# A decode kernel's five engine programs: in the bodies of a block, or straight in the main block

## The chip, the cores and the metric

The kernel runs on one core of a Trainium2 chip. Its time is the device time of one execution in microseconds (us). The profile's *span* is something else: it runs from the first to the last instruction of the program. What comes after the last instruction is in the time and not in the span (447.38 us against a span of 445.6 in the profiled execution of before). Some executions of this program fall into a slower state near 447 us; those are left out of every comparison of times. The one profile of the kernel before is of such a slow execution; where a reading rests on it, a fast profile is set beside it.

## The reference, cut to what matters

One decode step for 8 requests, condensed here: an adaptive layer norm whose six modulation vectors come from `silu(c) @ w_mod`, a grouped-query attention over a cache of 8192 keys and values (32 query heads, 4 key/value heads), and a gated feed-forward network.

```python
def reference(A_x, A_k_cache, A_v_cache, A_wq, A_wo, B_x, B_W_gate, B_W_up, B_W_down, c, w_mod):
    mod = (silu(c) @ w_mod).reshape(8, 6, 1, -1)             # sa, ca, ga, sb, cb, gb
    h = layernorm(A_x) * (1 + ca) + sa
    x = A_x + ga * attention(h, A_k_cache, A_v_cache, A_wq, A_wo)
    h = layernorm(x) * (1 + cb) + sb
    return x + gb * (relu(h @ B_W_gate) * (h @ B_W_up)) @ B_W_down
    # ... cut: the functions' bodies; all inputs and the output are bf16
```

Nearly all the data is read once: 185.63 MB from HBM, most of it the two caches.

## The kernel before: the parts that the argument touches

The kernel records every operation with what it reads and writes. `plan` turns dependencies into semaphore waits, and `emit` writes one engine's instructions.

```python
class Prog:
    ENGINES = ("sp", "act", "pool", "dve", "pe")
    # ... cut: op() finds each operation's dependencies, plan() numbers the semaphores
    def emit(self, eng, e, sems):
        known = {}
        for o in self.ops:
            if o["eng"] != eng:
                continue
            # ... cut: want = the semaphore values that o waits for
            for s, v in sorted(want.items(), key=str):
                if known.get(s, 0) < v:
                    known[s] = v
                    e.wait_ge(sems[s], v)
            # ... cut: the instructions themselves, and the increment of the last
```

Loads are issued by SyncE into a ring in SBUF; a load waits until the ring slot that it overwrites has been read. At the end of the program the result is stored by four DMAs, two issued by SyncE and two by ScalarE. SyncE then waits for all four. The last operation is empty: only its waits are emitted.

```python
        for j in range(4):
            P.op("sp" if j % 2 == 0 else "act",
                 lambda e, j=j: e.dma_start(o2[:, 256 * j:256 * (j + 1)], ob[32 * j:32 * j + B, :]),
                 reads=[R("ob")], writes=[("out", j, j + 1)], dma=True)
        P.op("sp", [], reads=[("out", 0, 4)])

        P.plan()
        block = E(nc.Block())
        bass_engs = {"sp": nc.sync, "act": nc.scalar, "pool": nc.gpsimd, "dve": nc.vector, "pe": nc.tensor}
        starters = {"sp": block.sync, "act": block.scalar, "pool": block.gpsimd, "dve": block.vector, "pe": block.tensor}
        for name in P.ENGINES:
            def body(_, name=name):
                P.emit(name, bass_engs[name], sems)
            starters[name](body)
```

`nc.Block()` gives each engine a body of its own. In the built program each engine has a branch into its body, a branch from the body's end to a common end block, and there a barrier of all engines: a drain and a semaphore wait on each, with GpSimd gathering the arrivals and releasing the rest.

Of the kernel before, what the change touches and what calls it, by code (L numbers as in the profile page):

```python
# [132 lines left out]
def bass_adaLN_cond__gqa_block_cached__glu_gated_reglu__decode_kernel(nc, A_x, A_k_cache, A_v_cache, A_wq, A_wo, B_x, B_W_gate, B_W_up, B_W_down, c, w_mod, out):  # L133
    B, _, D = A_x.shape
    _, G, Sk, Dh = A_k_cache.shape
# [16 lines left out]
    P = Prog()  # L152
    with ExitStack() as es:
        E = es.enter_context
# [50 lines left out]
        sems = {("eng", e): E(nc.semaphore("s_" + e)) for e in P.ENGINES}  # L205
# [417 lines left out]
        P.op("sp", [], reads=[("out", 0, 4)])  # L623

        P.plan()
        block = E(nc.Block())
        bass_engs = {"sp": nc.sync, "act": nc.scalar, "pool": nc.gpsimd, "dve": nc.vector, "pe": nc.tensor}
        starters = {"sp": block.sync, "act": block.scalar, "pool": block.gpsimd, "dve": block.vector, "pe": block.tensor}
        for name in P.ENGINES:
            def body(_, name=name):  # L630
                P.emit(name, bass_engs[name], sems)
            starters[name](body)


# [26 lines left out]
```

## Time and profile before

| | before |
|---|---|
| first three timed runs, us | 446.92, 439.91, 440.66 |
| profiled execution, us | 447.38, slow; span 445.6 |
| DMA | 185.90 MB at 417 GB/s over the span |

These lines of the page of the profiled execution of before say what bounds it. The digits of the DMA row are the busy share of the 16 DMA engines in tenths, in 40 equal slices of the span.

```profile
span 445.6 us, 4024 instructions
...
DMA  8999999999999999999999999999999999999994
...
DMA 48%; DVE 25%; PE 23%; ACT 2%; issue 1%; SPq 0%
...
L428 DVE STREAM_TRANSPOSE kt<-arena 128x1024 uint32<-128x1024 uint32 x128 | 148.6, 1215 | 44.6 <-DMA arena<-in_A_k_cache_dram 41.8
L439 PE MATMUL ps<-kt,qpad 128*128 128x512 bf16 x512 | 121.7, 382 | 12.7 <-DVE kt L428 10.8
```

The line with percentages is the chain of work that ended last. The lines of groups have busy us, mean ns of one instruction, then idle us before them and what ended it. The DMA engines are busy nearly throughout, and loads alternate on the chain with the work that frees their slots. Branches and barriers are not counted as work anywhere on this page.

The barriers do show among the waits of SyncE's queue in before: engine and line, what it waited for, total us, times, longest.

```profile
SPq L237 <- PE ps L482: 199.7, 16, 13.3
...
SPq L621 <- DVE ob L616: 34.2, 1, 34.2
...
SPq L123 <- DMA out_dram<-ob: 1.1, 2, 0.9
SPq L646 <- PEq L646: 0.7, 1, 0.7
SPq L153 <- PEq L153: 0.2, 1, 0.2
```

L123 is the wait for the stored result. L646 is the barrier at the start, which belongs to the launch code and not to the block. L153 is the end of the block. All instructions of the end of the block, in the trace of before, by source line (durations in ns, start of first and last in us):

```profile
L153 POOLq EVENT_SEMAPHORE  x2: 17/17/17, 445.4 to 445.5; - x2
L153 POOLq DRAIN  x1: 1024/1024/1024, 333.8 to 333.8; - x1
L153 PEldq DRAIN  x1: 462/462/462, 441.9 to 441.9; - x1
L153 DVEq DRAIN  x1: 464/464/464, 442.8 to 442.8; - x1
L153 ACTq DRAIN  x1: 234/234/234, 444.2 to 444.2; - x1
L153 SPq COMPARE_BRANCH  x1: 33/33/33, 445.2 to 445.2; - x1
L153 SPq DRAIN  x1: 7/7/7, 445.4 to 445.4; - x1
L153 SPq EVENT_SEMAPHORE  x1: 17/17/17, 445.5 to 445.5; - x1
L153 ACTq EVENT_SEMAPHORE  x1: 17/17/17, 445.5 to 445.5; - x1
L153 DVEq EVENT_SEMAPHORE  x1: 21/21/21, 445.5 to 445.5; - x1
L153 PEldq EVENT_SEMAPHORE  x1: 51/51/51, 445.5 to 445.5; - x1
```

### The profile page before, as it was taken

Reading aid. Unit: us, or ns where it says so; the run is one execution under the profiler, and the core shown is the slowest. Engines: PE = TensorE matmul, PEld = TensorE weight load, DVE = VectorE, ACT = ScalarE, POOL = GpSimd, SP = SyncE. Lnnn points to the kernel's source line nnn. Section 1 sums busy time; section 2 is a strip of 40 time slices with the busy share of each in tenths; the row PEclk is TensorE's granted clock in tenths of the full one; section 3 lists DMA queues with packets and bytes.
Section 4 is the critical chain, followed back from the end, with each engine's and each line's share of the span. In section 5 each row is a group of like instructions: output and inputs, shape, how many; then the busy total and the mean of one; then the engine's idle time right before and its main releaser. Section 6 shows DMA issues by size and latency. Waiting matters only on the chain.

```text
span 445.6 us, 4024 instructions
## 1 busy us (share of the span) xinstructions
PE 273.7 (61%) x1691; PEld 121.9 (27%) x1691; DVE 262.9 (59%) x372; ACT 28.8 (6%) x48; POOL 19.9 (4%) x77
## 2 busy tenths in 40 slices
PE   0054347585775959577595867769595875564235
PEld 0021112222332423333242333324233332351112
DVE  0233028396878769687885967788686878521020
ACT  1100010201001010110101011010101001100000
POOL 6000010000000000000000000000000000000000
PEclk9997557796969789696987969688796988867555
DMA  8999999999999999999999999999999999999994
GB/s 353 427 388 384 379 379 403 390 424 447 434 429 429 425 444 435 426 432 427 439 434 429 435 425 438 435 429 431 429 434 439 432 429 426 436 429 431 435 419 194
DMA packets 6946, 185.90 MB, mean 417 GB/s; under 512 B 816, under 2 KB 912, under 8 KB 1168
## 3 DMA queue, kind: packets, MB, share of 16 engines
q1 hardware_dynamic: 6896, 185.64, 98.4%
q8 instruction: 13, 0.21, 0.2%
q14 instruction: 5, 0.04, 0.0%
q10 hardware_dynamic: 32, 0.01, 0.0%
HBM read 185.63 MB, written 0.02 MB: 417 GB/s over the span
## 4 chain that ended last, share of the span: by engine, by line
DMA 48%; DVE 25%; PE 23%; ACT 2%; issue 1%; SPq 0%
DMA arena<-in_A_k_cache_dram 33%; DVE kt L428 14%; PE ps L482 11%; DMA arena<-in_B_W_down_dram 8%; PE ps L439 8%; DMA arena<-in_w_mod_dram 7%; DVE pT L473 4%; DVE negm L446 3%; ACT prb L466 2%; PE ps L571 1%; PE ps L352 1%; PE ps L452 1%; PE ps L592 1%; DVE mj L457 1%; DVE kt L561 0%
## 5 line engine op out<-in xcount | busy, mean ns | idle before, releaser
L428 DVE STREAM_TRANSPOSE kt<-arena 128x1024 uint32<-128x1024 uint32 x128 | 148.6, 1215 | 44.6 <-DMA arena<-in_A_k_cache_dram 41.8
L439 PE MATMUL ps<-kt,qpad 128*128 128x512 bf16 x512 | 121.7, 382 | 12.7 <-DVE kt L428 10.8
L482 PE MATMUL ps<-arena,pT 128*64 128x512 bf16 x512 | 92.1, 539 | 50.5 <-DVE pT L473 50.5
L482 PEld LDWEIGHTS ps<-arena,pT 128*64 128x64 bf16 x512 | 44.3, 153 | 92.9 <-issue 87.3
L439 PEld LDWEIGHTS ps<-kt,qpad 128*128 128x128 bf16 x512 | 45.1, 97 | 87.8 <-DVE kt L428 32.3
L473 DVE STREAM_TRANSPOSE pT<-prb 64x1024 bf16<-64x1024 bf16 x32 | 39.6, 1239 | 15.9 <-ACT prb L466 15.4
L466 ACT ACTIVATE prb<-ps,bias 128x1024 bf16<-128x1024 f32 x16 | 17.8, 1114 | 276.3 <-DVE mjt L460 276.3
L446 DVE TENSOR_REDUCE negm<-ps 128x1 f32<-128x512 f32 x32 | 22.0, 686 | 10.7 <-PE ps L439 10.5
L421 POOL COPY qpad<-qR 32x32 bf16<-32x32 bf16 x64 | 13.1, 204 | 314.0 <-PE ps L439 255.4
L592 PE MATMUL ps<-arena,hT 128*32 128x448 bf16 x128 | 11.2, 522 | 15.9 <-DMA arena<-in_B_W_gate_dram 6.8
L452 PE MATMUL ps<-identf,negm 128*128 128x128 f32 x32 | 7.8, 325 | 15.7 <-DVE negm L450 15.7
L495 DVE SCALAR_TENSOR_TENSOR om<-ps,im,om 128x128 f32<-128x128 f32 x48 | 16.7, 348 | 0.6
L375 PE MATMUL ps<-arena,hT 128*32 128x512 bf16 x64 | 7.2, 631 | 14.7 <-DMA arena<-in_A_wq_dram 14.7
L599 DVE TENSOR_TENSOR kt<-ps,kt 128x448 bf16<-128x448 f32 x2 | 1.2, 620 | 25.0 <-PE ps L592 25.0
L500 PE MATMUL ps<-jmp,om 128*128 128x16 f32 x32 | 6.5, 280 | 14.7 <-DVE om L495 14.7
L290 DVE CAST cxr<-ps 128x512 bf16<-128x512 f32 x1 | 0.7, 692 | 19.2 <-PE ps L288 19.2
L288 PE MATMUL ps<-cx,rsel 32*128 32x512 bf16 x1 | 0.6, 581 | 18.6 <-DMA cx<-in_A_x_dram 18.6
L385 DVE CAST kt<-ps 128x512 bf16<-128x512 f32 x1 | 0.7, 693 | 18.3 <-PE ps L375 18.3
L610 PE MATMUL ps<-arena,kt 128*32 128x256 bf16 x112 | 6.9, 416 | 7.4 <-DMA arena<-in_B_W_down_dram 7.3
L452 PEld LDWEIGHTS ps<-identf,negm 128*128 128x128 f32 x32 | 4.7, 187 | 23.6 <-DVE negm L450 22.1
L352 PE MATMUL ps<-arena,hT 128*32 128x512 bf16 x96 | 9.0, 553 | 2.4 <-DMA arena<-in_w_mod_dram 2.4
L592 PEld LDWEIGHTS ps<-arena,hT 128*32 128x32 bf16 x128 | 4.2, 129 | 22.2 <-DMA arena<-in_B_W_up_dram 8.3
(80 smaller groups left out, 95.7 us busy)
## 6 DMA issues: line engine op xcount, KB each, us to landing
arena<-in_A_k_cache_dram SPq DMA_DIRECT2D x16, 4096.0 KB, 28.9
arena<-in_A_v_cache_dram SPq DMA_DIRECT2D x16, 4096.0 KB, 25.7
arena<-in_w_mod_dram SPq DMA_DIRECT2D x2, 6144.0 KB, 17.4
arena<-in_A_wq_dram SPq DMA_DIRECT2D x2, 4096.0 KB, 25.0
arena<-in_A_wo_dram SPq DMA_DIRECT2D x2, 4096.0 KB, 27.5
arena<-in_B_W_gate_dram SPq DMA_DIRECT2D x2, 3584.0 KB, 30.5
arena<-in_B_W_up_dram SPq DMA_DIRECT2D x2, 3584.0 KB, 33.5
arena<-in_B_W_down_dram SPq DMA_DIRECT2D x1, 3584.0 KB, 36.1
```

Source lines behind the costliest of these rows:

```text
L352: fns.append(lambda e, w=w, pr=pr, j=j, kk=kk: e.matmul(ps[32 * j:32 * j + 32, pr, :], hT[:, kk, :], w[:, 2 * pr:2 * pr + 2, j, :], start= ...
L375: fns.append(lambda e, w=w, z=z, g=g, kk=kk: e.matmul(ps[32 * g:32 * g + 32, 3 + z, :], hT[:, kk, :], w[:, g, z, :], start=(kk == 0), stop ...
L421: P.op("pool", lambda e, n=2 * m + Q // 2, Q=Q: e.tensor_copy(qpad[32 * Q:32 * Q + 32, m % 2, :, 24 + 32 * Q:32 + 32 * Q], qR[32 * Q:32 * ...
L428: P.op("dve", lambda e: e.transpose(ktb[:, to:to + QE].bitcast(dt.uint32), arena[:, lo:lo + QE].bitcast(dt.uint32)), reads=[slot_r(lo, lo ...
L439: fns.append(lambda e, t=t, r=r: e.matmul(ps[:, b, :].rearrange("p (c k) -> p c k", k=32), qpad[:, m % 2, t * 2 + r, 24 - 8 * i:152 - 8 * ...
L446: P.op("dve", lambda e: e.tensor_reduce(negm[:, h:h + 1], ps[:, b, :], AX.X, ALU.max, negate=True), reads=[bank(b)], writes=[R("negm", h, ...
L452: P.op("pe", lambda e: e.matmul(ps[:, 4, 0:128], negm[:, 2:3].to_broadcast([128, 128]), identf[:], start=True, stop=True), reads=[R("negm" ...
L466: P.op("act", lambda e: e.activation(prb[:], ps[:, 2 * z:2 * z + 2, :].rearrange("p h n -> p (h n)"), ACT.Exp, bias=bias[:, z:z + 1], scal ...
L473: P.op("dve", lambda e, g=g: e.transpose(pT[64 * g:64 * g + 64, z, :, g, :], prb[64 * g:64 * g + 64, :]), reads=[R("prb"), R("pT", z, z + ...
L482: fns.append(lambda e, t=t: e.matmul(ps[64 * (t % 2):64 * (t % 2) + 64, 5, :].rearrange("p (i d) -> p i d", d=Dh), pT[:, z, t].rearrange(" ...
L495: P.op("dve", lambda e, i=i: e.scalar_tensor_tensor(out=om[:], in0=ps[:, 5, Dh * i:Dh * i + Dh], scalar=im[:, i:i + 1], in1=om[:], op0=ALU ...
L592: fns.append(lambda e, w=w, r=kk - r0, kk=kk, h=h, j=j, b0=b0: e.matmul(ps[32 * j:32 * j + 32, b0 + h, 0:H], hT[:, kk, :], w[:, r, j, h, : ...
```

## The change

The intent is to do without branches and without the barrier at the end. The program is the same otherwise: per engine, the same instructions in the same order.

```diff
         P.plan()
-        block = E(nc.Block())
-        bass_engs = {"sp": nc.sync, "act": nc.scalar, "pool": nc.gpsimd, "dve": nc.vector, "pe": nc.tensor}
-        starters = {"sp": block.sync, "act": block.scalar, "pool": block.gpsimd, "dve": block.vector, "pe": block.tensor}
-        for name in P.ENGINES:
-            def body(_, name=name):
-                P.emit(name, bass_engs[name], sems)
-            starters[name](body)
+        for name, e in (("sp", nc.sync), ("act", nc.scalar), ("pool", nc.gpsimd), ("dve", nc.vector), ("pe", nc.tensor)):
+            P.emit(name, e, sems)
```

## The prediction

> **What bounds the kernel now.** The span of the profiled run is 445.6 us (a slow-state run; timed: 439.91, 440.66 and one slow 446.92). The page gives 185.90 MB at a mean of 417 GB/s, DMA busy 8 or 9 tenths in 39 of 40 slices. The chain of what ended last is DMA 48%, DVE 25%, PE 23%: loads and the transposes and matmuls that free their ring slots take turns. "Issue" is 1%. No view gives a share to a branch or barrier; the change touches nothing of this bound.
>
> **What changes.** The comparison of the built programs shows the same instructions in the same order on each engine; the changed one lacks one unconditional branch per engine at the start, one at the end, and the end barrier (a drain and a semaphore wait on each engine, GpSimd gathering and releasing). The barrier at the start is not the block's, and stays. SyncE's waits for the four output DMAs stay as plain waits; the last rode on its branch. Nothing is added.
>
> **Cost at the end.** In the trace's instruction records SyncE's last output wait, on its branch, starts at 445.213 us and is done at 445.246; its drain is at 445.369, GpSimd's gather at 445.401, its release at 445.485, and the last engine leaves at 445.59. So 0.34 us follow the last output wait, all on the critical path. (The waits view has 0.2 us for SyncE there.) The other engines reach the barrier earlier (ScalarE's drain is done at 444.46), so their branches cost nothing. The runtime's own barrier afterwards (semaphore updates from 445.83 to 446.36), resets, and a second barrier until 447.51 stay.
>
> **Cost at the start.** SyncE's release from the first barrier ends at 0.673 us and its first load issues at 0.739: 0.066 us hold the branch and the issue gap. [...] TensorE's first matmul waits until 18.60 us for small input loads, so its branch is free.
>
> **Sum.** [...] From fast runs at about 440.3 I predict 439.9 us, range 438.8 to 443.0: run-to-run spread and a mix with slow-state runs exceed the effect. Chances: faster by over 2% 0.01, within 2% 0.97, slower 0.02.
>
> **What would show it.** SyncE's output wait is the last instruction, no end drain or gather; from last output DMA issue to the span's end about 0.35 us shorter; first load issue near 0.69 us instead of 0.74; all groups with the same counts and mean durations (transposes 1215 ns, score matmuls 382 ns); the same ring-slot waits on SyncE. Instruction fetches may move, without idle gaps on TensorE.
>
> **What would make it wrong.** The runtime's own barrier may absorb part of the 0.34 us, leaving 0.1 or nothing in the measured time though the span shrinks. [...] A median that falls on slow runs would read about 446.5, not the change's doing.

The sum came to about 0.4 us of 440, 0.1%: the 0.34 us of the end, and a second, smaller term for the branch at the start. That term was an assumed cost. The first load "near 0.69 us" rests on it too and on nothing that was measured. The names for what follows the program, a barrier of the runtime, resets and a second barrier, are the author's reading of semaphore updates; the trace shows the updates and their times.

## The result, and the profile after

| | before | changed |
|---|---|---|
| median of 6 runs, us | 440.65 (439.91 to 446.92) | 439.68 (439.07 to 440.08) |
| mean of the fast runs, us | 440.39 (5 runs) | 439.62 (6 runs) |
| ratio of fast runs | | 0.9982, 95% interval 0.9969 to 0.9996 |

Ratios are the mean time of one kernel's fast runs over that of the other's of the same rounds, so not quite the ratio of the medians. The changed kernel is faster by 0.2%, clear of noise but well within 2%. A second set of runs (e10) gave 0.9978 (0.9964 to 0.9991).

The page of the changed kernel has these lines in the places of those above.

```profile
span 438.7 us, 4012 instructions
...
DMA  8999999999999999999999999999999999999994
...
PE 35%; DMA 32%; DVE 26%; ACT 4%; issue 2%; SPq 1%
...
L428 DVE STREAM_TRANSPOSE kt<-arena 128x1024 uint32<-128x1024 uint32 x128 | 149.1, 1215 | 40.4 <-DMA arena<-in_A_k_cache_dram 33.1
L439 PE MATMUL ps<-kt,qpad 128*128 128x512 bf16 x512 | 120.8, 382 | 10.0 <-DVE kt L428 8.7
```

The work is the same to the nanosecond in its means (1215, 382). The 12 instructions by which the counts differ (4024, 4012) are the 12 listed at L153: 11 of the barrier and one branch. The two spans must not be subtracted: the profile of before is of a slow execution, this one of a fast one. The lag is not at the end of the program, where the change is; these stretches of before (in us: PE busy and count, then PEld, DVE, ACT and POOL, then clock, DMA share and GB/s) and then of the changed kernel show it in the first quarter.

```profile
0.00:112.00 112.00, 48.99 (x333) 19.80 (x334) 44.19 (x70) 8.86 (x15) 10.11 (x29) 0.79 0.99 397
112.00:400.00 288.00, 205.97 (x1117) 93.65 (x1115) 212.86 (x293) 18.75 (x30) 9.81 (x48) 0.84 1.00 432
```

```profile
0.00:112.00 112.00, 53.44 (x360) 22.44 (x361) 51.26 (x77) 8.86 (x15) 10.08 (x29) 0.85 0.99 425
112.00:400.00 288.00, 202.69 (x1124) 92.05 (x1122) 208.65 (x291) 18.95 (x31) 9.76 (x48) 0.83 1.00 432
```

397 against 425 GB/s in the first 112 us, and the same 432 afterwards. By the load issued at 111.66 us in before and at 105.26 in the changed kernel the lag is 6.4 us; at the first store (443.28 and 436.84) it is 6.4 us again. So it belongs to the state of that run: experiment e9 below, a fast-state profile of a kernel that still has block and barrier, issues that load at 105.12 us, level with the changed kernel.

The same waits of SyncE in the changed kernel; the line of the end barrier is gone, the others are as they were.

```profile
SPq L237 <- PE ps L482: 201.6, 16, 13.3
...
SPq L621 <- DVE ob L616: 35.3, 1, 35.3
...
SPq L123 <- DMA out_dram<-ob: 1.1, 2, 0.9
SPq L641 <- PEq L641: 0.7, 1, 0.7
```

The start did not move (0.739 us before, 0.736 changed; over all ten profiles the first load lies between 0.732 and 0.739, the lowest in e9, which has the block, and 0.739 again in e10, which has none). First issues of SyncE before, and then in the changed kernel (start us, us):

```profile
0.74 0.41 SPq L237 DMA_DIRECT2D arena<-in_w_mod_dram  x1
```

```profile
0.74 0.40 SPq L237 DMA_DIRECT2D arena<-in_w_mod_dram  x1
```

What did move is the end, and more of it than the span holds. The trace also has the updates of a semaphore that no instruction of the program names: 18 at the end in both traces, in two groups of nine (445.828 to 446.359 and 447.148 to 447.506 us in before). They are read here as two barriers by which the runtime synchronizes the engines once the program is done, and the single updates of 245 other semaphores (446.258 to 446.924 us in before) as its resets. The table sets the raw records side by side, in us from each trace's own start.

```
                                            before     changed
last output landing                        445.123     438.681
SyncE's last wait or branch done           445.246     438.725
last instruction done (end of span)        445.590     438.725
runtime's semaphore, update 1              445.828     436.067
                     update 2              445.862     438.103
                     update 3              446.074     438.142
                     update 4              446.117     438.186
                     update 5              446.141     438.846
                     update 9              446.359     439.009
                     last update           447.506     440.154
from last landing to last update             2.383       1.473
  of which up to the end of the span         0.467       0.044
  of which after the end of the span         1.916       1.429
recorded time of that execution             447.38      440.03
```

The recorded time ends 0.12 to 0.13 us before the last update in both, so in these two executions the time follows the last update. The tail, from the last landing of an output to the last update, is 0.91 us shorter: 0.42 us inside the span, and 0.49 us after it. That the profile of before is a slow one does not matter at this end: from SyncE's drain to the end of the span it has 0.22 us, and so have the fast profiles of e1 and e9, and its 1.916 us are those of e1. In the changed kernel the first four updates have happened before SyncE is done, because four engines no longer wait for it in a barrier. Which engine makes which update is inferred: in the changed kernel the first comes 0.19 us after TensorE's end, the second 0.36 after ScalarE's, the fifth 0.12 after SyncE's. e4, e5 and e8 test this reading.

### The profile page after: what moved, and what is told of

Read it like the earlier page. It is cut to its first block, busy times and chain, and to the rows that moved or that the text cites. A ratio compares the mean times of both kernels' runs of the same rounds, so it can differ in the third digit from the quotient of the medians.

```text
span 438.7 us, 4012 instructions
## 1 busy us (share of the span) xinstructions
PE 271.6 (62%) x1691; PEld 121.2 (28%) x1691; DVE 263.6 (60%) x372; ACT 28.8 (7%) x48; POOL 19.8 (5%) x77
## 4 chain that ended last, share of the span: by engine, by line
PE 35%; DMA 32%; DVE 26%; ACT 4%; issue 2%; SPq 1%
PE ps L482 18%; DMA arena<-in_A_k_cache_dram 15%; PE ps L439 13%; DVE kt L428 10%; DMA arena<-in_A_wq_dram 9%; DMA arena<-in_B_W_down_dram 8%; DVE pT L473 7%; DVE negm L446 4%; ACT prb L466 4%; PE ps L452 1%; PE ps L571 1%; DVE mj L457 1%; PE ps L375 1%; PE ps L592 1%; DVE mjt L460 1%
## 5 line engine op out<-in xcount | busy, mean ns | idle before, releaser
L428 DVE STREAM_TRANSPOSE kt<-arena 128x1024 uint32<-128x1024 uint32 x128 | 149.1, 1215 | 40.4 <-DMA arena<-in_A_k_cache_dram 33.1
L482 PE MATMUL ps<-arena,pT 128*64 128x512 bf16 x512 | 94.0, 547 | 51.1 <-DVE pT L473 51.1
L592 PE MATMUL ps<-arena,hT 128*32 128x448 bf16 x128 | 12.7, 577 | 14.5 <-DMA arena<-in_B_W_up_dram 6.8
L375 PE MATMUL ps<-arena,hT 128*32 128x512 bf16 x64 | 6.9, 608 | 13.9 <-DMA arena<-in_A_wq_dram 13.9
L610 PE MATMUL ps<-arena,kt 128*32 128x256 bf16 x112 | 6.0, 372 | 9.2 <-DMA arena<-in_B_W_down_dram 9.2
L500 PEld LDWEIGHTS ps<-jmp,om 128*128 128x128 f32 x32 | 5.0, 195 | 18.0 <-DVE om L495 16.9
```

The source lines that it names most:

```text
L375: fns.append(lambda e, w=w, z=z, g=g, kk=kk: e.matmul(ps[32 * g:32 * g + 32, 3 + z, :], hT[:, kk, :], w[:, g, z, :], start=(kk == 0), stop ...
L428: P.op("dve", lambda e: e.transpose(ktb[:, to:to + QE].bitcast(dt.uint32), arena[:, lo:lo + QE].bitcast(dt.uint32)), reads=[slot_r(lo, lo ...
L482: fns.append(lambda e, t=t: e.matmul(ps[64 * (t % 2):64 * (t % 2) + 64, 5, :].rearrange("p (i d) -> p i d", d=Dh), pT[:, z, t].rearrange(" ...
L500: P.op("pe", lambda e: e.matmul(ps[:, 6, 16 * m:16 * m + 16], om[:], jmp[:].rearrange("p g j -> p (g j)"), start=True, stop=True), reads=[ ...
L592: fns.append(lambda e, w=w, r=kk - r0, kk=kk, h=h, j=j, b0=b0: e.matmul(ps[32 * j:32 * j + 32, b0 + h, 0:H], hT[:, kk, :], w[:, r, j, h, : ...
```

## The experiments

The theory: the gain is the end barrier alone, twice over. It costs its own time after the last store, and it holds back four engines that could have gone through their part of the runtime's barrier while the stores were in flight. Rivals: the branches cost the time, by themselves or through the layout of instructions that they force; or the number of late engines matters and not which; or the difference is a faster load stream.

Times of single kernels scatter by about 0.4 us, as much as the effects. Each kernel has one profile; only the changed kernel has two, and its tail is 1.473 us in both. Each was also timed in five rounds beside before. All eight gave correct results; no run on record is labelled e6 or e7.

The record also gives the span of every timed run, to 0.1 us. The column "time minus span" is the mean of the recorded time minus that span over the fast runs, and it checks the middle part of the tail in runs whose traces were not kept. It is 1.74 to 1.85 us in each of the 21 fast runs of before (both later sets) and 1.26 to 1.37 in each of the 11 of the changed kernel: the half microsecond outside the span is there in every fast run.

| kernel | tail up to end of span, us | tail after it, us | whole tail, us | time minus span, us | mean of fast runs, us | ratio to before (95%) |
|---|---|---|---|---|---|---|
| before | 0.467 | 1.916 | 2.383 | 1.80 | 440.39 | |
| changed | 0.044 | 1.429 | 1.473 | 1.30 | 439.62 | 0.9982 (0.9969 to 0.9996) |
| e1 barrier, no block | 0.305 | 1.916 | 2.221 | 1.81 | 440.19 | 0.9991 (0.9979 to 1.0003) |
| e2 block, waits after it | 0.045 | 1.431 | 1.476 | 1.30 | 439.68 | 0.9979 (0.9967 to 0.9991) |
| e3 two barriers | 0.642 | 1.934 | 2.576 | 1.79 | 440.55 | 1.0000 (0.9987 to 1.0013) |
| e4 waits on TensorE | 0.079 | 1.680 | 1.759 | 1.57 | 439.57 | 0.9977 (0.9965 to 0.9989) |
| e5 waits on GpSimd | 0.067 | 1.994 | 2.061 | 1.86 | 440.00 | 0.9991 (0.9979 to 1.0003) |
| e8 barrier without GpSimd | 0.291 | 1.741 | 2.032 | 1.62 | 440.30 | 0.9998 (0.9986 to 1.0010) |
| e9 wait-free branch | 0.384 | 1.915 | 2.299 | 1.81 | 440.51 | 1.0003 (0.9989 to 1.0016) |
| e10 changed again | 0.045 | 1.428 | 1.473 | 1.31 | 439.41 | 0.9978 (0.9964 to 0.9991) |

e1 to e4 ran on one chip (before there: mean 440.54), e5 to e10 on another (before there: 440.37). The diffs of e2 and e9 are against the kernel before, the others against the changed kernel.

### e1: the barrier put back, without the block

```diff
             P.emit(name, e, sems)
+        nc.all_engine_barrier()
```

> The changed kernel with one all-engine barrier put back at the end, still without a block and so without branches. Theory (the gain is the end barrier: 0.34 us in the span, and about 0.5 us more because four engines then reach the runtime's own barrier only after SyncE): nearly all of the gain goes: fast-run mean 0.6 to 0.9 us above the changed kernel's 439.6, thus 440.3 +-0.3; from the last landing of an output to the runtime's last semaphore update 2.25 to 2.35 us (before 2.38, changed 1.47), time minus span back at about 1.8 us. Rival (the branches, or the layout of instructions that they force, cost the time): stays at 439.6, 1.47 us and 1.3 us.

Measured: tail 2.221 us, mean 440.19. The barrier without any branch brings back 0.75 of the 0.91 us: 0.26 us in the span and the whole 0.49 us after it. The tail came out just below the expected 2.25, and the mean just 0.57 us above the first set of the changed kernel (and 0.51 above e2, which ran on the same chip and has the changed kernel's tail). The missing 0.16 us lie between SyncE's last output wait and its drain; e9 takes them apart. The time minus span, 1.81 us, is back at that of before, as expected. The branches are not the main cost.

### e2: the block kept, the waits for the outputs behind it

```diff
-        P.op("sp", [], reads=[("out", 0, 4)])
         P.plan()
-        block = E(nc.Block())
+        with nc.Block() as block:
             # ... cut: the bodies as before
+        for o in P.ops[-4:]:
+            nc.sync.wait_ge(sems[o["sem"]], o["val"])
```

> The kernel before with its block, all ten branches and the end barrier; only SyncE's waits for the four outputs are moved behind the end barrier. Theory: the barrier then runs while the outputs are in flight, all engines but SyncE are early at the runtime's barrier, and the time is that of the changed kernel: ratio to before about 0.998, mean 439.6 +-0.4, from last landing to last runtime semaphore 1.45 to 1.6 us, time minus span about 1.3 us. Rival (branches or the number of instructions cost): stays at before, 440.4, with 2.2 to 2.4 us. First load issue near 0.74 us in any case.

Measured: tail 1.476 us, mean 439.68. This kernel is built with all ten branches and the whole barrier, and has the full gain. SyncE's waits in it:

```profile
SPq L633 <- DMA out_dram<-ob: 0.4, 2, 0.3
SPq L626 <- PEq L626: 0.4, 1, 0.4
```

The last engine to leave the barrier, and the waits for the stores, by line (the same columns as at L153 above):

```profile
L626 PEldq EVENT_SEMAPHORE  x1: 51/51/51, 437.8 to 437.8; - x1
...
L633 SPq EVENT_SEMAPHORE  x2: 28/28/28, 438.2 to 438.4; - x2
```

SyncE now spends 0.4 us in the barrier (L626) and 0.4 us waiting for the stores (L633), where it spent 0.2 and 1.1 us before. The barrier runs while the stores are in flight: it is over at 437.90 us, and the last output lands at 438.34. Moving four waits past the barrier does what deleting the block does, so neither the bodies' layout nor the branches at the start cost anything that the tail or the time shows. One thing moved along: SyncE's branch has lost its wait here, and no branch is in this trace at all. e9 looks at that one alone.

### e3: two barriers at the end

```diff
             P.emit(name, e, sems)
+        nc.all_engine_barrier()
+        nc.all_engine_barrier()
```

> The changed kernel with two all-engine barriers at the end. Theory: the second one adds its own 0.25 to 0.35 us of span and nothing in the runtime's part, since the first already made all engines late: landing to last runtime semaphore 2.5 to 2.7 us, time minus span still 1.8 us, mean 440.7 +-0.4. If each barrier made the runtime's part longer too, it would be about 3.1 us and 441.2.

Measured: tail 2.576 us, 0.36 us more than with one. The runtime's part stays (1.934 against 1.916). A barrier costs its own 0.26 to 0.36 us each time; the 0.49 us are paid once, for being late. The mean, 440.55, is as expected too, though the times alone would not show the difference.

### e4: the output waits on TensorE

```diff
-        P.op("sp", [], reads=[("out", 0, 4)])
+        P.op("pe", [], reads=[("out", 0, 4)])
```

> The changed kernel with the final waits for the outputs on TensorE instead of SyncE; no barrier. Reading of the runtime's barrier: its first semaphore updates come in the order TensorE, ScalarE, two others, SyncE. Theory: with TensorE the last to arrive, the whole first leg follows its arrival: time minus span 0.2 to 0.35 us above the changed kernel's 1.30, landing to last runtime semaphore 1.7 to 1.85 us, mean 439.9 +-0.4. If only the number of late engines mattered and not which, it stays at 1.47 us.

Measured: tail 1.759 us; after the end of the span 1.680 against 1.429. There is no barrier and no branch here, and exactly one engine is late, as in the changed kernel. It costs 0.25 us more. By the reading above, the first of the runtime's updates is TensorE's (it comes 0.19 us after TensorE's last instruction), and the others come only then: the ninth is 0.54 us after the end of the span, where it was 0.28 in the changed kernel. The mean, 439.57, is no slower than the changed kernel's: 0.29 us of tail is lost in the scatter of the times. The time minus span shows it in the timed runs too: 1.57 us (1.54 to 1.60) against 1.30.

### e5: the output waits on GpSimd

```diff
-        P.op("sp", [], reads=[("out", 0, 4)])
+        P.op("pool", [], reads=[("out", 0, 4)])
```

> The changed kernel with the final waits on GpSimd instead of SyncE; no barrier. In the traces so far the runtime's third semaphore update comes 0.57 us after GpSimd's last instruction, whenever GpSimd was late (before, one barrier, two barriers), while SyncE's fifth comes 0.12 us after SyncE's and TensorE's first 0.19 us after TensorE's. Theory (which engine is late decides, and GpSimd is the slow one to enter): from the end of the span to the runtime's last update 1.95 to 2.05 us (changed 1.43, waits on TensorE 1.68), landing to last update 2.0 to 2.15 us, mean 440.1 +-0.4. Rival (the number of late engines decides): as with TensorE, 1.68 us.

Measured: tail 2.061 us; after the end of the span 1.994, as the theory had it. Updates 1 and 2 have come by 437.291 us; the third comes 0.53 us after GpSimd's last instruction (0.56 to 0.57 in before, e1, e2 and e3; TensorE's update follows its last instruction by 0.19 to 0.24, SyncE's by 0.12), and the fourth and fifth within 0.07 us of it. The time minus span is 1.86 us, the longest of all. So of the three engines tried GpSimd is the costliest to have last. What it does in that half microsecond no record shows.

### e8: a barrier of four engines, without GpSimd

```diff
             P.emit(name, e, sems)
+        nc.multi_engine_barrier([x.engine for x in (nc.sync, nc.scalar, nc.vector, nc.tensor)])
```

> The changed kernel with a barrier of SyncE, ScalarE, VectorE and TensorE at the end; GpSimd takes no part and is long done. Theory: what the barrier costs in the runtime's part falls from 0.49 to about 0.25 us, for GpSimd is not late: end of span to the runtime's last update 1.6 to 1.75 us (all-engine barrier 1.92, changed 1.43), span part of the barrier 0.2 to 0.3 us, landing to last update 1.9 to 2.05 us. Rival (any barrier makes the runtime's part 0.49 us longer): 1.92 us and 2.2 us.

Measured: tail 2.032 us; up to the end of the span 0.291, nearly the all-engine barrier's 0.305, and after it 1.741 instead of 1.916. With GpSimd out of the barrier, the third update follows the second at once (439.094 after 439.056). GpSimd's lateness is thus 0.18 of the 0.49 us, and that of the others the rest. The mean, 440.30, did not improve on e1's 440.19, measured on the other chip; that is inside the scatter. The time minus span did: 1.62 us against 1.81.

### e9: before, with SyncE's branch freed of its wait

```diff
-        P.op("sp", [], reads=[("out", 0, 4)])
+        P.op("sp", [lambda e: e.nop(nofuse=True)], reads=[("out", 0, 4)])
```

> The kernel before, with block, branches and end barrier, with a no-op of SyncE behind its waits, which the build drops: what is left of it is that the four output waits sit on two wait instructions as in the changed kernel and SyncE's branch has no wait of its own. Before, SyncE took 0.20 us from the end of the last wait instruction to its drain, with the branch recorded in between; with the barrier and no branch, 0.05 us. Theory (a branch costs only where it carries a wait; the others are not executed as instructions): no branch in the records, 0.05 us, landing to last runtime update 2.2 to 2.25 us, mean 440.2 to 440.6. Rival [...]: a branch record, or 0.1 us and more before the drain, and 2.28 to 2.38 us.

The rival held that a branch costs time in itself.

Measured: tail 2.299 us. This is over the expected 2.2 to 2.25 and inside the range that was given to the rival, 2.28 to 2.38; the branch record and the time before the drain fall on the theory's side. These are SyncE's lines at the end of the block in e9, in place of three in before:

```profile
L153 SPq DRAIN  x1: 7/7/7, 438.6 to 438.6; - x1
L153 SPq EVENT_SEMAPHORE  x1: 17/17/17, 438.7 to 438.7; - x1
```

No branch is recorded any more: without a wait to carry, SyncE's branch leaves no record and no time that shows, since SyncE's drain follows its last wait by 0.046 us in e9 as in e1, which has no branches. In before it was 0.202 us from the last plain wait, with the branch in between. The expectation missed one thing: in e9 the wait for the store that landed last sits on the first of the two wait instructions, so the second still follows it. The records from the last landing to the drain are 0.246 us in before (wait, branch, drain), 0.164 in e9 (wait, wait, drain) and 0.090 in e1 (wait, drain). A further instruction behind the last landing costs 0.07 us, and the branch with a wait, in its place, 0.08 us more. So the rival was right about this one branch, and about no other. The 0.08 us come from the one profile of before, which is slow; its first two steps (0.017 us from the landing to the first of these instructions, 0.073 to the next) are those of e9 (0.016, 0.074). The first load of e9 is issued at 0.732 us, against 0.736 in the changed kernel, so its branches at the start cost nothing that shows.

### e10: the changed kernel again

The same file as after the change, with nothing edited.

> The changed kernel once more, beside before on this chip, to set the experiments against it: mean 439.4 to 439.9, ratio 0.997 to 0.999, landing to last runtime update 1.45 to 1.50 us, time minus span 1.25 to 1.35 us.

Measured: mean 439.41, ratio 0.9978, tail 1.473 us. In this set, before's mean is 0.96 us higher; in the first it was 0.78. The tail's 0.91 lies between.

No version beat the changed kernel clearly: of the three engines tried SyncE, which it uses, is the cheapest to leave waiting (1.43 us after the end of the span, against 1.68 with TensorE and 1.99 with GpSimd; ScalarE and VectorE were not tried), and e2 only equals it. Whether fewer stores at the end would shorten what precedes the tail was not tried.

## Why the prediction was right, and where it was not

- **What bounds the kernel, and that the change leaves it alone: right.** Transposes 1215 ns and score matmuls 382 ns before and after, the same waits for ring slots, 432 GB/s in the steady part.
- **The cost at the end of the span: right in kind, somewhat small.** Predicted were 0.34 us after SyncE's last wait, put down to the barrier; nothing follows that wait in the changed kernel. Measured from the last landing, 0.42 us went from the span's tail; e1 and e9 divide it into 0.26 us of barrier and 0.16 us for the branch and the instruction slot that it took. So the barrier itself was taken too large, by about 0.08 us that the branch cost, and the rest of the branch's cost was left out.
- **The start: wrong, by a small amount.** The saving was to show as a first load near 0.69 us. It came at 0.736 instead of 0.739, and from the end of SyncE's release to that load there are 0.065 us without the branch, where there were 0.066 with it. The branches at the start leave no record; in e9 SyncE's branch at the end lost its record with its wait, so the only branch that shows in any trace here is one with a wait of its own. The forecast charged an assumed cost to something that cost no time that shows here. Nor do the instruction queues tell the kernels apart: 13 and 5 packets within the span in both.
- **The sum: its largest term was missing.** The prediction held that the runtime's barrier, resets and second barrier "stay", and among its doubts that the barrier "may absorb part of the 0.34 us". The opposite holds: the runtime's part after the span fell by 0.49 us, because its barrier was no longer queued behind the kernel's own. e2 (1.431 us with a barrier that ends before the stores land) against e1 (1.916) isolates it. The gain was 0.91 us by the tail and 0.78 and 0.96 us by the means, where 0.4 was predicted. What a late engine does to the rest is the question that leads to the missing term. From the end of the span to the ninth update these runs have 0.28 us with SyncE alone late, 0.54 with TensorE alone, 0.82 with GpSimd alone, 0.60 with all but GpSimd and 0.77 with all five.
- **The time:** 439.68 against 439.9, inside the range. The range, 438.8 to 443.0, would have held an unchanged 440.3 too, so being inside it says little about the sum: the gain was about twice the 0.4 us that the sum gave, and still 0.2%.
- **Slow runs:** none fell among the changed kernel's six, so the upper part of the range was not needed. Before had one of six here, and none and one of eleven in the two later sets; e3 had one of six, e9 two of six. The runs are too few to tie this to anything.

## What to carry to other kernels

In these runs a barrier at the end of a kernel cost twice: its own 0.26 to 0.36 us after the last store, and the head start that idle engines would have had into what is read here as the runtime's closing barrier (0.49 us with all five engines held back). If a barrier is needed at all, put it before the wait for the last stores, and leave only SyncE to wait for these; e2 had the whole gain that way (a tail of 1.476 us, against 1.473 in the changed kernel). Compare the recorded time with the span when a change touches the end of a program, for half of this gain (0.49 of 0.91 us) lies outside the span, and count instructions in the trace and not in the program, for nine of the ten branches left no record and no time that shows.
